# The head of the load queues: a first quarter of x in two token halves, and weight rows ahead of the DMA transposes

## Chip, cores, metric

One NeuronCore of one Trainium2 chip. The metric is the device time of one execution in microseconds (us). Kernels were timed in rounds beside the kernel before on the same chip.

## The reference

```python
# x (1, 2048, 1024), w_gate and w_up (1024, 3584), w_down (3584, 1024), all bf16
def reference(x, w_gate, w_up, w_down):
    return (_gelu(x @ w_gate) * (x @ w_up)) @ w_down   # gelu: the tanh form
```

## The kernel before

It computes the three products with a seven-product block scheme and is bound by TensorE for nearly the whole time. The change touches only the first 10 us: how the first 512 tokens of x and the first weight columns come in. The contraction has eight rows of 128 (`kd` 0 to 7). Rows 0 to 3 of x are loaded as they are, in two quarters of 256 columns, and transposed on TensorE; rows 4 to 7 come through DMA transposes. Weight columns 0 to 255 of a chunk come first (rows 0-1, 2-4, 5-7), columns 256 to 511 (here "the second column halves") after them.

```python
    FA = 2 * P
    first = (0, 0)
    load_x0(0, sp)                       # first quarter of x, 256 KB
    load_w(first, 0, 0, 2, act, 0, FA)   # gate rows 0-1 (j = 0 is gate, 1 is up)
    load_w(first, 1, 0, 2, sp, 0, FA)
    load_x0(1, act)                      # second quarter
    load_w(first, 0, 2, 5, act, 0, FA)
    load_w(first, 1, 2, 5, sp, 0, FA)
    act(nc.scalar.preload_act_table(ACT.Gelu_apprx_tanh))
    # ... (cut: identity)
    for i in range(NWARM):               # NWARM = 8 warm-up matmuls
        pe(nc.tensor.matmul(banks[i][:], lhsT=warm_l, rhs=warm_r, start=True, stop=True))

    for kd in range(KH, KD):             # x rows 4 to 7, one DMA transpose each
        load_xT(xT, 0, 0, kd, kd + 1)
        if kd == KH + 1:
            for j in range(2):
                load_w(first, j, 5, KD, act, 0, FA)
    for j in range(2):
        load_w(first, j, 0, KD, sp, FA, FG)   # the second column halves
    # ... (cut: second token block, next chunk)

    def first_units(hT):                 # columns 0-255, units 0 and 1
        wg, wu = chunks[first]
        held = (VB, RB)
        transpose_x0(0)                  # TensorE, rows 0 and 1; copies to SBUF on VectorE
        for kd, j in [(kd, j) for kd in range(KD) for j in range(2)]:
            for u in range(2):
                mm_gu(banks[held[u][j]], (wg, wu)[j], u, 0, kd)
            if (j, kd) == (1, 0):
                transpose_x0(1)          # rows 2 and 3; copies on VectorE and ACT
        for u in range(2):
            unit_out(hT, held[u], u, 0)
    # ... then unit 2 and 3: the second column halves
```

## Time and profile before

| | before |
|---|---|
| time, median of 3 runs (range) | 542.07 us (541.71 to 542.49) |
| span of the profiled execution | 539.7 us |
| first transposes on TensorE | 4.38 us |
| second transposes | 6.10 us |
| unit 2 begins | 13.07 us |

Times within a profile count from the start of its span. Where I give the start of one matmul or the landing of one load, it is from the records of the trace; a load has landed when the last of its engines has reported, and these reports come over up to 2.5 us. A line of a timeline gives start and length in us, the engine (PE TensorE's matmuls, PEld its weight loads, DVE VectorE, ACT ScalarE, SPq and ACTq the issuing of those two queues), the source line, the operation, what it writes <- reads, the shapes, how many, and in brackets the idle time before it and what ended that. One line that the readings below need is not in the prediction, the second transposes:

```profile
6.10 0.61 PE L302 MATMUL bank<-ident,w_mem 128*128 128x128 bf16 x8
```

### The profile page before, as it was taken

Reading aid. Unit: us, or ns where it says so; the run is one execution under the profiler, and the core shown is the slowest. Engines: PE = TensorE matmul, PEld = TensorE weight load, DVE = VectorE, ACT = ScalarE, POOL = GpSimd, SP = SyncE. Lnnn points to the kernel's source line nnn. Section 1 sums busy time; section 2 is a strip of 40 time slices with the busy share of each in tenths; the row PEclk is TensorE's granted clock in tenths of the full one; section 3 lists DMA queues with packets and bytes.
Section 4 is the critical chain, followed back from the end, with each engine's and each line's share of the span. In section 5 each row is a group of like instructions: output and inputs, shape, how many; then the busy total and the mean of one; then the engine's idle time right before and its main releaser. Section 6 shows DMA issues by size and latency. Waiting matters only on the chain.

```text
span 539.7 us, 7102 instructions
## 1 busy us (share of the span) xinstructions
PE 535.1 (99%) x2392; PEld 374.5 (69%) x2392; DVE 354.9 (66%) x466; ACT 258.9 (48%) x438; POOL 235.0 (44%) x206
## 2 busy tenths in 40 slices
PE   9999999999999999999999999999999999999997
PEld 3457777666776676767776677777777766866865
DVE  1767777787775997889574434444444469969951
ACT  2435555555555319216465555555555551452270
POOL 0197777777776000000056776666777730000000
PEclk9999999999999999999999999999999999999999
DMA  9928577696827876779950405041331466677946
GB/s 233 310 82 230 185 242 237 184 286 195 277 76 252 299 244 227 249 265 313 327 182 1 155 2 156 7 149 57 99 106 51 157 204 213 226 241 246 291 145 207
DMA packets 84771, 102.70 MB, mean 190 GB/s; under 512 B 18688, under 2 KB 66304, under 8 KB 84736
## 3 DMA queue, kind: packets, MB, share of 16 engines
q1 hardware_dynamic: 61936, 80.30, 46.2%
q10 hardware_dynamic: 22800, 21.96, 13.2%
q8 instruction: 19, 0.31, 0.2%
q14 instruction: 16, 0.13, 0.1%
HBM read 85.98 MB, written 12.58 MB: 183 GB/s over the span
## 4 chain that ended last, share of the span: by engine, by line
PE 98%; DMA 1%; ACTq 0%; ACT 0%; issue 0%
PE bank L386 61%; PE bank L656 33%; PE bank L252 5%; DMA w_mem<-in_w_gate_dram 1%; ACTq L161 0%; ACT xT L312 0%; ACT o_sb L709 0%; ACTq L167 0%; ACTq L709 0%
## 5 line engine op out<-in xcount | busy, mean ns | idle before, releaser
L386 PE MATMUL bank<-t_mem,s_mem 128*128 128x512 f32 x1016 | 239.8, 394 | 0.0
L386 PEld LDWEIGHTS bank<-t_mem,s_mem 128*128 128x128 f32 x1016 | 190.8, 188 | 41.9
L358 POOL TENSOR_TENSOR s_mem<-w_mem 128x512 fp32r<-128x512 bf16 x100 | 115.8, 1178 | 201.3 <-DMA w_mem<-in_w_up_dram 104.6
L276 DVE TENSOR_TENSOR hT<-w_mem,bank 128x512 bf16<-128x512 f32 x104 | 71.3, 686 | 92.4 <-PE bank L386 46.3
L656 PE MATMUL bank<-t_mem,s_mem 128*128 128x512 f32 x544 | 127.2, 392 | 0.0
L656 PEld LDWEIGHTS bank<-t_mem,s_mem 128*128 128x128 f32 x544 | 102.1, 188 | 22.2 <-issue 0.2
L409 DVE TENSOR_TENSOR bank<-bank,m 128x512 f32<-128x512 f32 x104 | 67.3, 694 | 46.9 <-ACT m L431 45.3
L386 PE MATMUL bank<-xT,w_mem 128*128 128x512 bf16 x416 | 94.3, 380 | 0.0
L271 ACT ACTIVATE w_mem<-bank 128x512 f32<-128x512 f32 x104 | 61.9, 596 | 57.7 <-DVE bank L409 32.7
L386 PEld LDWEIGHTS <-w_mem 128*128 128x128 bf16 x416 | 38.7, 98 | 49.7 <-issue 6.5
L566 DVE TENSOR_TENSOR t_mem<-w_mem 128x1024 fp32r<-128x1024 bf16 x56 | 65.5, 1216 | 0.0
L358 POOL TENSOR_TENSOR s_mem<-w_mem,s_mem 128x512 fp32r<-128x512 bf16 x50 | 62.1, 1267 | 0.0
L358 POOL TENSOR_TENSOR s_mem<-s_mem,w_mem 128x512 fp32r<-128x512 f32 x50 | 59.6, 1212 | 0.0
L371 ACT CAST s_mem<-w_mem 128x512 fp32r<-128x512 bf16 x52 | 32.0, 616 | 33.1 <-PE bank L386 29.1
L436 ACT COPY bank<-bank 128x512 f32<-128x512 f32 x52 | 29.6, 570 | 38.1 <-PE bank L386 38.1
L631 DVE TENSOR_TENSOR s_mem<-hT 128x512 fp32r<-128x512 bf16 x52 | 34.2, 685 | 10.2 <-PE bank L656 9.5
L656 PEld LDWEIGHTS <-hT 128*128 128x128 bf16 x224 | 21.3, 98 | 26.6 <-issue 2.1
L431 ACT COPY m<-bank 128x512 f32<-128x512 f32 x52 | 30.5, 587 | 17.1 <-PE bank L386 17.1
L440 ACT COPY bank<-bank 128x512 f32<-128x512 f32 x52 | 29.6, 570 | 13.5 <-PE bank L386 13.5
L709 ACT CAST o_sb<-bank 128x512 bf16<-128x512 f32 x28 | 15.4, 585 | 39.6 <-PE bank L656 39.6
L591 DVE TENSOR_TENSOR o_sb<-wd_sb,o_sb 128x512 fp32r<-128x512 bf16 x28 | 29.4, 1051 | 0.5
L252 PE MATMUL bank<-xT,w_mem 128*128 128x512 bf16 x128 | 28.4, 379 | 0.3 <-DVE xT L310 0.2
(42 smaller groups left out, 250.4 us busy)
## 6 DMA issues: line engine op xcount, KB each, us to landing
t_mem<-t_dram SPq DMA_DIRECT2D x56, 512.0 KB, 5.3
w_mem<-in_w_gate_dram ACTq DMA_DIRECT2D x10, 1024.0 KB, 5.6
w_mem<-in_w_up_dram ACTq DMA_DIRECT2D x10, 1024.0 KB, 9.1
wd_sb<-in_w_down_dram SPq DMA_DIRECT2D x28, 256.0 KB, 5.0
t_dram<-o_sb SPq DMA_DIRECT2D x28, 256.0 KB, 2.4
wd_sb<-in_w_down_dram SPq DMA_DIRECT2D x12, 512.0 KB, 8.8
w_mem<-in_w_down_dram SPq DMA_DIRECT2D x10, 512.0 KB, 6.1
w_mem<-in_w_down_dram SPq DMA_DIRECT2D x4, 1024.0 KB, 6.3
```

The source lines that it names most:

```text
L252: nc.tensor.matmul(ps[:], lhsT=w_sb[:, kd, fi * P : (fi + 1) * P], rhs=xT[tb][:, kd, :], start=(kd == 0), stop=(kd == KD - 1),)
L271: act(nc.scalar.activation(out=g_sb, in_=ps[:], func=ACT.Gelu_apprx_tanh))
L276: nc.vector.tensor_tensor(out=hT[:, fc, tb * TB : (tb + 1) * TB], in0=g_sb, in1=ps[:], op=ALU.mult,)
L358: pool(nc.gpsimd.tensor_tensor(out=t, in0=in0, in1=in1, op=op))
L371: act(nc.scalar.copy(out=t, in_=a(1, 1)))
L386: nc.tensor.matmul(banks[bank][:], lhsT=lhs[:, c, :], rhs=rhs[:, c, :], start=start and c == 0, stop=c == KH - 1, skip_group_check=True,)
L409: nc.vector.tensor_tensor(out=banks[dst][:], in0=banks[src][:], in1=m5[j][:], op=ALU.add)
L431: act(nc.scalar.copy(out=m5[j][:], in_=banks[V_[j]][:]))
L436: act(nc.scalar.copy(out=banks[RB[j]][:], in_=banks[QB[j]][:]))
L566: dve(nc.vector.tensor_tensor(out=t, in0=in0, in1=in1, op=ALU.subtract))
L631: dve(nc.vector.tensor_tensor(out=t, in0=in0, in1=in1, op=op))
L656: nc.tensor.matmul(banks[bset[u]][:], lhsT=lhs(i, u), rhs=rhs(i), start=start and i == 0, stop=stop and i == NS - 1, skip_group_check=True,)
```

## The change

The intent: start TensorE earlier, by giving each queue only half of the first quarter of x at its head, and keep ACT from stopping, by issuing weight rows 5 to 7 before the DMA transposes. One warm-up matmul is dropped, as real work should come sooner. To make room, the second quarter of x goes from second place on ACT to third on SP.

```diff
-    NWARM = 8
+    NWARM = 7
# ...
-    def load_x0(q, queue):
+    def load_x0(q, queue, ts0=0, ts1=TSB):
         eng = nc.scalar if queue is act else nc.sync
         cols = slice(q * XQ, (q + 1) * XQ)
-        src = x2[0:TB, cols].rearrange("(ts p) d -> p ts d", p=P)
-        queue(eng.dma_start(out=xs0[:, :, cols], in_=src))
+        src = x2[ts0 * P : ts1 * P, cols].rearrange("(ts p) d -> p ts d", p=P)
+        queue(eng.dma_start(out=xs0[:, ts0:ts1, cols], in_=src))
# ...
-    load_x0(0, sp)
+    load_x0(0, sp, 0, 2)
+    load_x0(0, act, 2, 4)
+    load_w(first, 1, 0, 2, sp, 0, FA)
     load_w(first, 0, 0, 2, act, 0, FA)
-    load_w(first, 1, 0, 2, sp, 0, FA)
-    load_x0(1, act)
+    load_x0(1, sp)
     load_w(first, 0, 2, 5, act, 0, FA)
     load_w(first, 1, 2, 5, sp, 0, FA)
+    for j in range(2):
+        load_w(first, j, 5, KD, act, 0, FA)
     act(nc.scalar.preload_act_table(ACT.Gelu_apprx_tanh))
 # ...
     for kd in range(KH, KD):
         load_xT(xT, 0, 0, kd, kd + 1)
-        if kd == KH + 1:
-            for j in range(2):
-                load_w(first, j, 5, KD, act, 0, FA)
```

## The prediction

> **What bounds the kernel now.** I read the page first: the busy shares and the chain that ended last, for how much of the time the change can touch at all. TensorE is busy for 535.1 of 539.7 us and is 98% of the chain; loads of the gate weights are 1%.
>
> ```profile
> span 539.7 us, 7102 instructions
> PE 535.1 (99%) x2392; PEld 374.5 (69%) x2392; DVE 354.9 (66%) x466; ACT 258.9 (48%) x438; POOL 235.0 (44%) x206
> PE 98%; DMA 1%; ACTq 0%; ACT 0%; issue 0%
> ```
>
> The change touches only loads issued before the loop and one warm-up matmul. So the second view is the timeline of the first 30 us. What the reader is to see: the warm-up matmuls, whose weight loads come every 0.43 us; the first real work at 4.38, when the first quarter of x has landed; the first weight matmul at 5.24; and, from 6.55 on, 107 matmuls in 23.74 us, or about 0.22 us each, which is nearly the gap of 0.216 us between two such matmuls that nothing holds up. From 10.9 us on no gap is left in the raw starts.
>
> ```profile
> 0.77 3.43 PE L202 MATMUL bank<-const-bfloat16-1.0 128*128 128x512 bf16 x8 [0.77 <-PEq L961]
> 2.29 5.12 SPq L172 DMA_TRANSPOSE xT<-in_x_dram  x4
> 4.38 0.62 PE L302 MATMUL bank<-ident,w_mem 128*128 128x128 bf16 x8 [0.18 <-DMA w_mem<-in_x_dram]
> 5.24 1.02 PE L252 MATMUL bank<-xT,w_mem 128*128 128x512 bf16 x4 [0.24 <-DVE xT L310]
> 6.55 23.74 PE L252 MATMUL bank<-xT,w_mem 128*128 128x512 bf16 x107
> 7.46 0.58 SPq L161 DMA_DIRECT2D w_mem<-in_w_gate_dram  x1
> 8.71 7.33 SPq L172 DMA_TRANSPOSE xT<-in_x_dram  x2
> ```
>
> Third, the chain in order of time for 0 to 15 us. What the reader is to see: the ACT queue stops. It issues gate rows 2 to 4 at 1.82, these land 5.65 us later at 7.47, only then does ACT issue the up rows 5 to 7 (7.50), and only behind that issue does ACT make the PSUM copy (7.98) that feeds the matmuls of row 3.
>
> ```profile
> 1.82 5.65 DMA w_mem<-in_w_gate_dram
> 7.50 0.44 ACTq L161
> 7.98 0.59 ACT xT L312
> 8.61 6.57 PE bank L252 x29
> ```
>
> Fourth, the waits from 4 to 14 us, to size what TensorE itself loses.
>
> ```profile
> PEld L252 <- DMA w_mem<-in_w_up_dram: 0.5, 1, 0.5
> PEld L252 <- DMA w_mem<-in_w_gate_dram: 0.4, 1, 0.4
> ```
>
> A weight load runs ahead of its matmul, so these waits are larger than what TensorE loses. From the single matmul starts against the 0.216 us step I get three holes: 0.12 before 7.53 (gate row 2), 0.21 before 8.61 (the ACT copy), 0.14 before 10.90 (up row 5). In sum **0.47 us**. That, and the start at 4.38, is all that this change can win: the later 510 us are TensorE back to back.
>
> **What the skill says, and whether the trace agrees.** "DMA: Bandwidth & Descriptors", Anatomy of one DMA: a transfer has a fixed part of about 2.0 us beside bytes over bandwidth. The trace agrees in kind: in the DMA view of the first microsecond 256 KB of x land after 3.6 us and 128 KB of gate after 3.4 us, so halving the bytes hardly shortens one. The same page, Issuing engines are not separate DMA queues: loads from SP and ACT run on the same 16 engines, and issuing on both saves only issue time. Issues here cost 0.45 to 0.58 us each, so that is what two halves at the heads of two queues may save. "TensorE: Matmul & The Clock Gate", Part 1: the array runs at half rate until a window of about 3.4 us has been busy, and the window is free-running. The trace agrees: warm-up steps are 0.43 us, twice 0.216, and the clock record goes to full at 3.92. The first page's Rules for kernel authors say that a transpose beside ordinary DMAs needs nothing; so the waits below are of the program's semaphores, not of the crossbar.
>
> **The change, part by part.**
> (a) The first quarter of x. Before, 256 KB led SP and 128 KB of gate led ACT; 384 KB had landed by 4.34. Now the two heads are 128 KB each and nothing else is ahead. The DMA view shows about 0.2 MB moved by 3.0 us and some 340 GB/s after that, so 256 KB have moved by about 3.2; the lag from bytes to landing is about 0.7. Estimate: 3.9 to 4.0, transposes at 3.95, **0.4 us earlier**. The first weights move to second place: issued at 1.24, landing after 3.5 as the second SP load does today, at 4.75. They are needed 0.86 us after the transposes (4.38 to 5.24 today), at 4.8, so they don't cost.
> (b) One warm-up matmul less: seven end at 0.77 + 7 x 0.43 = 3.8. Without this the eighth would hold TensorE until 4.2 and eat half of (a). Worth nothing by itself.
> (c) The second quarter goes from second on ACT to third on SP (issue 1.74 instead of 1.24). Needed after the first four matmuls, at 4.8 + 0.86 = 5.7; it landed at 5.5 with as many bytes ahead. No cost.
> (d) The last weight rows (5 to 7) on ACT before its table load. Gate rows go out at about 2.4 without a wait. All DMA landings of the trace come on eight semaphores, and an issue from the ninth on waits for the transfer eight before it: ACT's issue at 4.36 sits on the landing of x at 4.34, the one at 7.50 on that of gate rows 2 to 4 at 7.47. The up rows are now the ninth or tenth issue and wait for one of the two halves, until 4.0, not 7.5. So ACT is free by 5.8 (table load 1.28) for the copy needed near 7, and all **0.47 us** of holes go. First units alone could then end 0.4 + 0.47 = 0.9 us earlier: unit 2 at 12.2 instead of 13.07.
> (e) What it takes away. The four transposes of x rows 4 to 7 begin at 2.29 today. They now stand behind nine weight and x loads in the count of eight semaphores, so the first waits for a landing, until about 4.0, and four issues at 1.26 us (2.29 to 7.41 today) end at 9.1. Everything behind them on SP is 1.6 us later: the second column halves of gate and up, issued at 7.46 and 8.09 today, go at 9.1 and 9.7. They land 5.1 and 6.3 us after issue today, at 12.54 and 14.35, against use at 13.07 and 14.80: **0.53 and 0.45 us of slack**. They share the engines then with 192 KB of up rows that now go before, so they will be quicker: data start about 1.5 us after issue, 10.7, 512 KB at about 310 GB/s are 1.7 us, and 0.75 of lag, so gate at about 13.1 and up at about 14.85. These are estimates from the trace's packets.
>
> The sum: TensorE reaches unit 2 at 12.2 but its weights at 13.1, and the up half at 14.85 instead of 14.80. The 0.9 us won in (a) and (d) become a wait for the second column halves. **Net about 0, by my central estimate a gain of 0.1 to 0.2 us**, as the 1.6 us delay may be partly hidden in the queue. Later parts have room: the second x block, some 1.6 us later, lands near 18 and 20, for use at 19.98 and 20.84; GpSimd's first sums, started by weights that come at 22.8 and 25.8, end their second step at 31.85 for use at about 36.
>
> **The rivals.**
> 1. The gain is kept. The transposes don't wait, or the second halves are limited by bandwidth and not by issue, so that bytes moved earlier bring them earlier. For it: 16 engines show 250 to 310 GB/s almost without a hole from 2 to 14 us. Against it: their data start right behind the last transposes (9.5), which are held by 1.26 us each of issue. It would give up to 0.9 us: 541.2.
> 2. The wait moves and grows. The last transposes come late (issue at 7.8 plus the 3.7 us of today is 11.5, needed at 11.3) and the second halves come with the whole 1.6 us: 14.1 and 15.9, against 13.07 and 14.80. That costs 1.1 us: 543.2.
> 3. The clock. Seven warm-ups and a pause of 0.15 us may miss the window, and TensorE runs at half rate for up to another 3.4 us: at most 1.7 us lost, 543.8. For it: the flip at 3.92 is only 0.16 after the seventh ends. Against it: nine tenths of the window are busy. I give it one in ten.
> 4. Nothing of it, in that 3.8 us of warm-up and the DMA's fixed part hold the start: transposes at 4.2 or later. Then the start gives 0.2.
>
> **The range and the chances.** The centre is 542.07 - 0.15 = 541.9. Three runs before lie 0.8 us apart, and rivals 1 and 2 stand 0.9 below and 1.1 above; with weights of a quarter and a sixth the range of 8 in 10 is 541.1 to 542.9. Two per cent are 10.8 us, more than the whole 8.6 us up to row 3's matmuls, and all holes I found are 0.9; only a mistake such as a lost overlap in the later 500 us could do that. So same 0.99, faster 0.005, slower 0.005.
>
> **What would show it.** In the changed profile: transposes near 3.95 and first weight matmul near 4.8 (a); the ACT copy near 7 and no hole before rows 2, 3 and 5 (d); the first DMA transpose at about 4.0 and the second column halves issued about 9.1 (e); and a wait of weight loads for gate or up just before units 2, of 0.5 us or more. It is wrong if that wait is missing and TensorE reaches unit 2 near 12.2 (rival 1), if it stands at rows 6 and 7 (rival 2), or if matmul steps after 4 us are 0.43 us (rival 3).

## The result, and the profile after

| | before | after |
|---|---|---|
| time, median of 4 runs (range) | 542.28 us (541.71 to 542.76) | 542.90 us (542.53 to 543.79) |
| ratio after/before, 95% interval | | 1.0013 (0.9993 to 1.0033) |
| span of the profiled execution | 539.7 us | 540.7 us |

A ratio is the mean time of one kernel's runs over that of the other's of the same rounds, so it is not quite the ratio of the medians. The interval holds 1: by time alone the change is "same". The median stands at the very top of my range, 1.0 above its centre, and where I forecast a gain of 0.15 us there is a loss of about 0.6. The traces say more than the times.

The timeline of the changed kernel, lines that answer to those of before:

```profile
0.77 3.14 PE L205 MATMUL bank<-const-bfloat16-1.0 128*128 128x512 bf16 x7 [0.77 <-PEq L961]
...
3.72 5.11 SPq L172 DMA_TRANSPOSE xT<-in_x_dram  x4
...
3.75 1.07 PE L302 MATMUL bank<-ident,w_mem 128*128 128x128 bf16 x8
...
4.87 1.48 PE L252 MATMUL bank<-xT,w_mem 128*128 128x512 bf16 x4
...
6.47 0.62 PE L302 MATMUL bank<-ident,w_mem 128*128 128x128 bf16 x8
...
7.13 0.58 ACT L312 COPY xT<-bank 128x512 bf16<-128x512 bf16 x1 [1.45 <-PE bank L302]
8.88 0.58 SPq L161 DMA_DIRECT2D w_mem<-in_w_gate_dram  x1
...
13.54 10.75 PE L252 MATMUL bank<-xT,w_mem 128*128 128x512 bf16 x49 [0.21 <-DMA w_mem<-in_w_gate_dram]
```

The first transposes come 0.63 us earlier (3.75 against 4.38) and ACT's copy comes at 7.13, not 7.98. But the second transposes come 0.37 us later (6.47 against 6.10), and unit 2 begins at 13.54 against 13.07, after a wait for the gate half. The start gained 0.63 us, yet by unit 2 the kernel is 0.47 us behind.

The chain in order of time (of the whole run; its first part) shows what released unit 2. In the kernel before it ran through ACT's stopped queue; here it runs through SP's transposes, and ACT is gone from it:

```profile
0.74 2.96 DMA w_mem<-in_x_dram
3.70 0.02 issue
3.72 1.22 SPq L172
...
7.57 1.26 SPq L172
8.83 0.04 issue
8.88 4.62 DMA w_mem<-in_w_gate_dram
13.50 0.05 issue
13.54 20.90 PE bank L252 x96
```

The first DMA transpose waits for the first half of x (landed at 3.70), four issues follow, then the gate half of the second columns, 4.62 us in flight.

The table by stretches tells the same from the DMA side (the last two columns are the busy share of the DMA engines, which can pass 1, and GB/s). First the kernel before, then the changed one:

```profile
10.00:11.00 1.00, 1.00 (x6) 0.30 (x5) 0.00 (x0) 0.00 (x0) 0.00 (x0) 1.00 1.14 324
```

```profile
10.00:11.00 1.00, 1.00 (x6) 0.42 (x5) 0.00 (x0) 0.00 (x0) 0.00 (x0) 1.00 0.63 80
```

Between 10 and 11 us the engines move 80 GB/s, not 324. So bandwidth did not hold the gate half back there: it had been issued late, at 8.88, and by the packets of the trace its data came in bulk only from about 10.6.

Behind unit 2 the two traces run in step until 129 us, where the changed kernel loses another 0.41 us (0.47 becomes 0.88 at the last matmul). The waits from 125 to 131 us have one line there that the kernel before lacks, VectorE waiting for the store of a staged transpose:

```profile
DVE o_sb L591 <- DMA x_dram<-o_sb: 1.9, 1, 1.9
```

### The profile page after: what moved, and what is told of

Same layout as the page of the kernel before. It is cut to its first block, busy times and chain, and to the rows that moved or that the text cites. A ratio compares the mean times of both kernels' runs of the same rounds, so it can differ in the third digit from the quotient of the medians.

```text
span 540.7 us, 7104 instructions
## 1 busy us (share of the span) xinstructions
PE 535.9 (99%) x2391; PEld 374.7 (69%) x2391; DVE 356.5 (66%) x466; ACT 258.7 (48%) x438; POOL 235.1 (43%) x206
## 4 chain that ended last, share of the span: by engine, by line
PE 93%; DMA 4%; DVE 1%; SPq 1%; issue 0%; ACT 0%; DVEq 0%; ACTq 0%
PE bank L386 56%; PE bank L656 33%; PE bank L252 4%; DMA o_sb<-in_x_dram 2%; SPq L172 1%; DMA w_mem<-in_w_gate_dram 1%; DVE o_sb L591 1%; DMA w_mem<-in_x_dram 1%; DMA t_dram<-o_sb 0%; DMA x_dram<-o_sb 0%; DVE s_mem L631 0%; DVE bank L409 0%; ACT o_sb L709 0%; SPq L593 0%; ACT w_mem L271 0%
```

## The experiments

Theories at the start: **A**, the second column halves come late since the transposes ahead of them on SP wait for one of eight semaphores; **B**, the missing warm-up matmul delays the full clock; **C**, the loss at 129 us belongs to the change. After the first four runs came **D**: the second quarter of x comes late because of its new place. Twelve kernels were run; all gave correct results.

### after_again: the changed kernel unchanged

> The changed kernel once more, unchanged, for what repeats. Theory A (the second column halves of gate and up come late, because the DMA transposes ahead of them on SP wait for one of eight semaphores): first transpose issued near 3.7 us, halves at 8.9 and 9.5, gate half landing near 13.5, a hole of 0.3 to 0.5 us before unit 2, in this profile too. Rival B (the clock goes full at 5.8 instead of 3.9 because a warm-up matmul is missing): the flip is near 5.8 again; if it was only the phase of the window, it will stand elsewhere between 3.8 and 7.2. Rival C (a wait near 129 us costs 0.4 us more because staging is late): the same step of +0.4 there again. Time 1.000 to 1.003 of the kernel before.

Ratio 1.0016 (0.9989 to 1.0042). Issue of transposes and halves repeats: 3.62, 8.98. But unit 2 has no hole in front of it and begins at 14.37, 1.3 us later than before. The loss sits in another place, in front of the second transposes. Timeline:

```profile
4.71 1.04 PE L252 MATMUL bank<-xT,w_mem 128*128 128x512 bf16 x4 [0.30 <-DMA w_mem<-in_w_gate_dram]
7.63 0.45 PEld L302 LDWEIGHTS <-w_mem 128*128 128x128 bf16 x8 [2.38 <-DMA w_mem<-in_x_dram]
7.63 0.62 PE L302 MATMUL bank<-ident,w_mem 128*128 128x128 bf16 x8 [1.89 <-DMA w_mem<-in_x_dram]
```

TensorE is done with its first four matmuls by 5.75 and stands 1.89 us until the second quarter has landed (7.59). In the first profile the same load landed at 6.42, but the half-rate clock stretched the first matmuls to 6.35 (1.48 us instead of 1.04), so most of the wait was hidden: the fourth matmul began at 5.97, one step of 0.216 later TensorE could have gone on, and it went on at 6.47, so about 0.28 us were seen. That is the term I had put at zero. The gate half then lands at 13.95, before TensorE needs it: the two losses don't add, the longer one counts. The clock went full at 3.79 here, so the 5.80 of the first profile was not fixed by the seven matmuls.

### after_w8: eight warm-up matmuls

```diff
-    NWARM = 7
+    NWARM = 8
```

> The change with eight warm-up matmuls as before. Theory A: no difference at unit 2: its first matmul stays near 13.5, since it waits for a landing; TensorE just waits a little longer or shorter there. Rival B: if the missing matmul delays the clock, the flip is back at 3.9, the first units end 0.4 to 0.9 us earlier, but unit 2 starts at 13.5 all the same if A holds; only if A is false does the time fall by 0.5 us or more.

Ratio 1.0007 (0.9983 to 1.0030). Clock full at 4.26. Second quarter landed at 6.95, a wait of 0.92 us at the second transposes (7.00); gate half at 13.75, unit 2 at 13.80 with a hole of 0.30. As A says, an early clock doesn't help: unit 2 begins when the gate half lands.

### after_fa_act: the second column halves on ACT

```diff
         load_w(first, j, 5, KD, act, 0, FA)
+    for j in range(2):
+        load_w(first, j, 0, KD, act, FA, FG)
     act(nc.scalar.preload_act_table(ACT.Gelu_apprx_tanh))
 # ...
-    for j in range(2):
-        load_w(first, j, 0, KD, sp, FA, FG)
```

> The change with the second column halves of gate and up moved from SP (behind the DMA transposes) to ACT (behind rows 5 to 7, ahead of the table load). Theory A (issue-bound): they are issued near 4.4 to 5.5, land before 12, the hole before unit 2 is gone and unit 2 starts at 12.3 to 12.9, so 0.6 to 1.2 us earlier than in the changed kernel; or the hole moves to rows 4 to 7, if the transposes now come late. Bandwidth rival: the sum of bytes is the same, the halves still land at 12.5 to 13.5 and rows 4 to 7 come later than now, so nothing is won or some is lost.

A miss, and the largest loss: ratio 1.0063 (1.0040 to 1.0086). The timeline:

```profile
5.02 0.37 ACTq L161 DMA_DIRECT2D w_mem<-in_w_gate_dram  x1
...
8.96 0.43 ACTq L161 DMA_DIRECT2D w_mem<-in_w_up_dram  x1
...
10.72 0.58 ACT L312 COPY xT<-bank 128x512 bf16<-128x512 bf16 x1
...
11.36 3.61 PE L252 MATMUL bank<-xT,w_mem 128*128 128x512 bf16 x16 [1.56 <-ACT xT L312]
15.42 1.89 PE L252 MATMUL bank<-xT,w_mem 128*128 128x512 bf16 x8 [0.45 <-DMA xT<-in_x_dram]
```

ACT's second issue waits for a semaphore until 8.96, the table load and the copy behind it come late (the copy at 10.72) and hold TensorE by 1.56 us. The last transpose, issued at 8.39 instead of 7.57 and now in flight beside the halves, lands only at 15.38, too late for row 7. The gate half, issued at 5.02, needed 7.7 us and landed at 12.72. So an early issue alone did not bring it before 12 here. Why it needed 7.7 us stays open: bandwidth alone doesn't explain it, as the DMA view shows mostly 35 to 185 GB/s from 7.2 to 9 us, against 280 to 360 from 5.2 to 7.1.

### after_rows_back: rows 5 to 7 back behind the second transpose

```diff
-    for j in range(2):
-        load_w(first, j, 5, KD, act, 0, FA)
     act(nc.scalar.preload_act_table(ACT.Gelu_apprx_tanh))
 # ...
         load_xT(xT, 0, 0, kd, kd + 1)
+        if kd == KH + 1:
+            for j in range(2):
+                load_w(first, j, 5, KD, act, 0, FA)
```

> The change with rows 5 to 7 put back behind the second DMA transpose, the halves of x kept at the heads of the queues. Theory A: only seven loads stand before the first transpose, so it is issued near 2.8 without a wait and the second near 4.0; the second column halves go near 7.9, land near 12.6, and unit 2 starts at 12.6 to 13.1, some 0.5 to 0.9 us before the changed kernel. If what costs is the split of x itself (second quarter late, landing at 6.4), then unit 2 stays at 13.3 or later.

Ratio 1.0004 (0.9978 to 1.0029). SP's timeline:

```profile
2.80 5.11 SPq L172 DMA_TRANSPOSE xT<-in_x_dram  x4
...
7.96 0.58 SPq L161 DMA_DIRECT2D w_mem<-in_w_gate_dram  x1
```

With seven loads ahead the first transpose needs no semaphore back and goes at 2.80, the halves at 7.96; the gate half lands at 12.87 and unit 2 begins at 13.03 without a hole. That is A's forecast, but for a gate half 0.3 us later than its 12.6. The start is as early as in the changed kernel (3.71), yet unit 2 is only 0.04 us before that of the kernel before: at half rate until 6.42, the first four matmuls took 1.79 us and the second transposes began at 6.49. The second quarter, landed at 6.05, held nothing here.

### before_again: the kernel before unchanged

> The kernel before once more, for what repeats. If the second quarter of x lands late in the changed kernels because of its place in the queues (theory D), it lands here by 5.8 on its last engine again (5.52 in the first profile; 6.05 to 7.59 in five profiles with the new order). If it is just how the engines straggle on a given execution, it lands here anywhere from 5.5 to 7.5. Second column half of gate issued near 7.5, landing near 12.5, no hole before unit 2; unit 2 at 12.9 to 13.6. Clock flip anywhere from 3.8 to 7.2.

Ratio 0.9986 (0.9961 to 1.0011). Second quarter at 5.65, second transposes at 6.25, halves issued at 7.45, gate half at 12.36, no hole, unit 2 at 12.77. D's number; and the spread of the kernel before at unit 2 is at least 0.3 us, as gate rows 2 to 4 happened to land early and ACT held nothing.

### before_rows: only rows 5 to 7 ahead of the transposes

```diff
     load_w(first, 1, 2, 5, sp, 0, FA)
+    for j in range(2):
+        load_w(first, j, 5, KD, act, 0, FA)
     act(nc.scalar.preload_act_table(ACT.Gelu_apprx_tanh))
 # ... and taken out behind the second transpose
```

> The kernel before with only one part of the change: weight rows 5 to 7 issued ahead of the DMA transposes; x whole, eight warm-ups. Theory A: the first transpose waits for a landing until about 4.1 to 4.4, the second column halves go at 9.3 to 9.6 and the gate half lands near 13.8; no hole at rows 3 and 5, but one of 0.5 us or more before unit 2, which starts near 13.8, so this part alone costs 0.5 to 0.8 us. Second quarter of x lands by 5.8 (theory D: its place is the old one). If the loss were of the split of x only, unit 2 would start at 12.6 here.

Ratio 0.9985 (0.9964 to 1.0006). Partly a miss: here the first transpose still got a free semaphore (it was the seventh or eighth issue) and went at 2.30, only the second waited, until 4.24. The halves went at 8.12, 0.67 later than before, the gate half landed at 12.97, unit 2 began at 13.28 and waited for nothing. The second quarter, in its old place, landed at 5.63, as D wants. What held TensorE back was the clock, at half rate until 6.38. So this part alone costs nothing that shows, but its delay uses up most of the slack of the halves (gate landed at 12.97; the kernel before used it at 13.07).

### x1_act: the second quarter third on ACT

```diff
-    load_x0(1, sp)
+    load_x0(1, act)
```

> The change with the second quarter of x moved back to the ACT queue (third there), nothing else. Theory D by place: it has 256 KB ahead in its ring still, so it lands at 5.8 to 6.5, hardly better; by straggling beside the deeper ACT queue: it lands at 5.4 to 5.7. Theory A: second halves issued near 8.4 to 8.9, hole before unit 2 stays; unit 2 near 13.0 to 13.6.

A miss: ratio 1.0003 (0.9978 to 1.0028). It lands at 7.14, later than either forecast, its first engine as late as 6.26; TensorE waits 1.28 us at the second transposes (7.19) and unit 2 begins at 13.83, though the gate half, issued at 7.75, had landed at 12.77. Third place is late on ACT too, though not alike: here all engines are late, on SP mainly the last ones (below).

### x1_split: the second quarter in halves, third on both queues; rows 5 to 7 back

```diff
-    load_x0(1, sp)
+    load_x0(1, sp, 0, 2)
+    load_x0(1, act, 2, 4)
 # rows 5 to 7 as in after_rows_back
```

> The second quarter of x split in two token halves as well, third on each queue, and rows 5 to 7 back behind the second transpose. Theory D: each ring has only 256 KB ahead and 128 KB of it, so the quarter lands by 5.6, and with a warm clock the second transposes of TensorE run right after the first four matmuls, near 5.6 to 5.8. Eight loads are then ahead of the first DMA transpose, which waits until 3.7 (theory A), so the second halves go at 8.9 and unit 2 starts at 13.2 to 13.6 all the same. If A is wrong, unit 2 starts at 12.2 to 12.6.

Ratio 1.0009 (0.9985 to 1.0034). The halves land at 5.89 and 6.26, the earliest but one of the third places, though later than I expected; TensorE's second transposes run from 5.93, the last six from 6.31. Eight loads are ahead, the first transpose waits until 3.97, the halves go at 9.13, and the timeline has the hole before unit 2 again:

```profile
13.70 1.41 PEld L254 LDWEIGHTS <-w_mem 128*128 128x128 bf16 x8 [0.74 <-DMA w_mem<-in_w_gate_dram]
13.70 2.55 PE L254 MATMUL bank<-xT,w_mem 128*128 128x512 bf16 x11 [0.25 <-DMA w_mem<-in_w_gate_dram]
```

With D nearly mended, unit 2 still waits for the gate half: A alone is enough to hold it until 13.70.

### after_xt2: two DMA transposes of two rows instead of four of one

```diff
-    for kd in range(KH, KD):
-        load_xT(xT, 0, 0, kd, kd + 1)
+    for kd in range(KH, KD, 2):
+        load_xT(xT, 0, 0, kd, kd + 2)
```

> The changed kernel with its four DMA transposes of one x row each joined into two of two rows. The later transposes of four rows take 1.6 to 2.3 us to issue where nothing blocks them, so two of two rows should take some 3 us or less instead of 5.1. Theory A (the second column halves are late by their issue, landing 4.5 to 5.1 us after it, in nine profiles): first transpose still waits until near 3.7, the halves go by about 6.5 instead of 8.9, the gate half lands before 12.0, and no hole is left before unit 2. Theory D: the second quarter of x still lands at 6.0 to 7.6, so unit 2 starts at 12.6 to 13.9. If landing is bound by bandwidth instead, the gate half still lands at 12.8 or later.

A miss in size. Ratio 1.0009 (0.9993 to 1.0024). The second transpose took 3.30 us to issue, so the halves went at 7.98, not 6.5, and the gate half landed at 13.37; rows 4 and 5 came as one transfer at 10.74, a wait of 0.76 us for TensorE; unit 2 began at 14.2 (worked out from ACT's third gelu less 1.93 us, as this trace lacks some matmul records). The second quarter landed at 6.77, so D holds; A is not tested by it, since little of the issue time went away.

### x1_second: the second quarter second on SP

```diff
+    load_x0(1, sp)
     load_w(first, 1, 0, 2, sp, 0, FA)
     load_w(first, 0, 0, 2, act, 0, FA)
-    load_x0(1, sp)
```

> The changed kernel with the second quarter of x put second on SP, ahead of the first up rows; nothing else. Theory D (place in the ring: 128 KB ahead as in the kernel before, not 256 KB): it lands at 5.2 to 5.8 on its last engine; the first up rows, third now, land at 5.6 to 6.5 and TensorE waits up to 1 us for them instead. If it straggles for another reason, it lands at 6.0 to 7.6 as in the other new orders. Second halves issued near 8.9, landing near 13.5, unit 2 near 13.5.

Ratio 1.0016 (1.0003 to 1.0029). It lands at 5.25, the earliest of all, with everything else of the change in place. So one place further up mends it, as D says. The price stands in the timeline:

```profile
5.52 1.89 PE L252 MATMUL bank<-xT,w_mem 128*128 128x512 bf16 x4 [0.73 <-DMA w_mem<-in_w_gate_dram]
...
7.20 1.06 PE L302 MATMUL bank<-ident,w_mem 128*128 128x128 bf16 x8
```

The first gate rows now land at 5.47 instead of 4.8, TensorE stands 0.73 us, and its clock stays at half rate until 9.93 (the four matmuls take 1.89 us, the transposes 1.06). Unit 2 begins near 15.0, not near 13.5 as expected. Whether the pause caused the late clock, one profile can't say.

### before_x1_late: only the place of the second quarter

```diff
-    load_x0(1, act)
     load_w(first, 0, 2, 5, act, 0, FA)
+    load_x0(1, act)
```

> The kernel before with one thing of the change alone: the second quarter of x goes from second to third place in its queue (ACT), behind gate rows 2 to 4; x whole, eight warm-ups, rows 5 to 7 where they were. Theory D (place): it lands at 6.2 to 7.3 on its last engine instead of 5.5 to 5.7, TensorE waits 0.4 to 1.3 us before its second transposes (they begin at 6.3 to 7.4 instead of 6.10), and unit 2 starts at 13.2 to 14.0 instead of 12.8 to 13.1. If place doesn't matter and the head halves make the engines straggle, it lands by 5.8 and unit 2 starts at 12.7 to 13.1.

Its interval lies just above 1, as that of x1_second does: ratio 1.0027 (1.0004 to 1.0049); with a bound of 2% both count as the same. From the timeline:

```profile
5.39 1.29 PE L252 MATMUL bank<-xT,w_mem 128*128 128x512 bf16 x4
...
6.99 0.62 PE L302 MATMUL bank<-ident,w_mem 128*128 128x128 bf16 x8 [0.32 <-DMA w_mem<-in_x_dram]
```

It lands at 6.95, the second transposes wait for it until 6.99 (6.10 before), and unit 2 begins at 13.50. With nothing else of the change, the new place makes the load late by 1.4 us. Two things keep this from being the lateness of the changed kernel: the clock, at half rate until 5.96, would have put the second transposes at about 6.5 by itself, and here the load has 192 KB more ahead of it in all, not only in its queue, so that already its first engine is 1.6 us late (6.77 against 5.17).

### before_xt2_dve: a version meant to beat both

The kernel before with two-row transposes, rows 5 to 7 issued behind both of them, and row 3's copy on VectorE.

```diff
-    for kd in range(KH, KD):
-        load_xT(xT, 0, 0, kd, kd + 1)
-        if kd == KH + 1:
-            for j in range(2):
-                load_w(first, j, 5, KD, act, 0, FA)
+    for kd in range(KH, KD, 2):
+        load_xT(xT, 0, 0, kd, kd + 2)
+    for j in range(2):
+        load_w(first, j, 5, KD, act, 0, FA)
 # ...
-            if q == 0 or n == 0:
+            if True:
```

> A version meant to beat both: the kernel before, with its queue heads and second quarter as they are, the four DMA transposes joined into two, and the PSUM copy for row 3 on VectorE instead of ACT, so that a blocked ACT queue holds no matmul. Theory: second quarter of x lands by 5.7; no hole before row 3; second halves issued by about 6.0, gate half landing by 11.5; rows 4 and 5 of x may come later as one transfer, needed at 9.4. Unit 2 starts at 12.4 to 12.8, 0.3 to 0.6 us before the kernel before; time 0.998 to 1.000 of it, which the timing alone can't resolve here.

Not resolved. Median 541.81 beside 542.42 of the kernel before, five of six runs between 541.1 and 544.7, one at 547.59; ratio 1.0016 (0.9981 to 1.0052). Halves issued at 6.70, gate half landed at 12.45 (5.8 us in flight, so no earlier than before), unit 2 at 12.8. It is not shown to beat the kernel before.

### All looks side by side

One profile each; us from the start of the span. "Place" is that of the second quarter of x in its queue. Unit 2 of x1_second, after_xt2 and before_xt2_dve is worked out from ACT's third gelu.

| kernel | place | it lands | second transposes | gate half issued | lands | unit 2 | clock full |
|---|---|---|---|---|---|---|---|
| before | 2, ACT | 5.52 | 6.10 | 7.46 | 12.54 | 13.07 | 3.92 |
| before_again | 2, ACT | 5.65 | 6.25 | 7.45 | 12.36 | 12.77 | 4.22 |
| before_rows | 2, ACT | 5.63 | 6.79 | 8.12 | 12.97 | 13.28 | 6.38 |
| before_xt2_dve | 2, ACT | 5.54 | 6.24 | 6.70 | 12.45 | 12.8 | 4.79 |
| x1_second | 2, SP | 5.25 | 7.20 | 9.26 | 14.16 | 15.0 | 9.93 |
| before_x1_late | 3, ACT | 6.95 | 6.99 | 7.45 | 12.54 | 13.50 | 5.96 |
| after_rows_back | 3, SP | 6.05 | 6.49 | 7.96 | 12.87 | 13.03 | 6.42 |
| x1_act | 3, ACT | 7.14 | 7.19 | 7.75 | 12.77 | 13.83 | 3.97 |
| after | 3, SP | 6.42 | 6.47 | 8.88 | 13.49 | 13.54 | 5.80 |
| after_w8 | 3, SP | 6.95 | 7.00 | 8.89 | 13.75 | 13.80 | 4.26 |
| after_again | 3, SP | 7.59 | 7.63 | 8.98 | 13.95 | 14.37 | 3.79 |
| x1_split | 3, both | 5.89, 6.26 | 5.93, 6.31 | 9.13 | 13.66 | 13.70 | 5.27 |
| after_xt2 | 3, SP | 6.77 | 6.82 | 7.98 | 13.37 | 14.2 | 5.47 |
| after_fa_act | 3, SP | 7.40 | 7.45 | 5.02 (ACT) | 12.72 | 16.28 | 5.21 |

Five looks at second place: 5.25 to 5.65. Eight looks at an unsplit third place: 6.05 to 7.59. The ranges don't touch.

## Why the prediction was wrong

Two steps failed. Each alone is enough to undo the gain, and which of them ends last differs from look to look.

**The last term of (e), the flight of the second column halves.** In the profile beside the result, unit 2 began 0.05 us after the gate half had landed, so this term set it. The mechanism was right: the first transpose waited for a landing, the halves were issued late, and unit 2 got a hole. The size was not. I let the flight shrink from 5.1 us to 4.0, as the halves would have less company. It took 4.62 us (4.86 and 4.97 in after_w8 and after_again). So the gate half, though issued at 8.88 and not 9.1, landed at 13.49 and not 13.1, and a loss of 0.47 us stood at unit 2 where I had none.

**(c)**, "It landed at 5.5 with as many bytes ahead. No cost." It landed at 6.42 to 7.59 in three looks (after, after_again, and after_w8 with eight warm-ups). The cost at the second transposes was about 0.28 us in the first profile, 0.92 in after_w8 and 1.89 in after_again, and in the last of these it, and not the gate half, set unit 2. I counted the bytes issued ahead over both queues, 512 KB in both kernels. This fits its first engine: it reported at 5.27, against 5.17 before. It fails for the last one, at 6.42 against 5.52. In the six looks at third place on SP, unsplit (after, after_again, after_w8, after_fa_act, after_rows_back, after_xt2), the first engine reported at 4.90 to 5.42, and the last one 0.6 to 2.5 us after it, against 0.35 in the kernel before.

That the new place makes the load late is shown: one place further up mends it (x1_second), and the ranges of the table don't touch. By what it does so is in part argued. In the kernel before, 128 KB stood ahead of it in ACT's queue, now 256 KB in SP's. The Trainium skill's "DMA: Bandwidth & Descriptors", Queues, rings and completion order, fits: each engine takes turns between the queues' rings, packet by packet, and consumes one ring in order; I quoted the same page for the shared engines and left this out. The packets of the traces, counted without regard to the engine (they don't name it), agree: when as many bytes of its queue had gone out as end with this load, both queues together had moved 806 to 828 KB in the four looks at second place on ACT, 868 to 931 KB at third on SP, 1005 in x1_act, 1200 in before_x1_late and 628 in x1_second. So before_x1_late and x1_second move more than the place in one queue: in both, the bytes in its own queue, those in all and the moment of issue (1.75 instead of 1.24 in the change) move together. By the same count these bytes were out 0.3 to 0.8 us later than before; the rest of the loss on SP is the tail of late engines. Why some engines lag so is not settled.

**Right: (a)**, in kind and nearly in size. Transposes at 3.75 instead of 3.95 as forecast; gain 0.63 instead of 0.4. First gate rows at 4.82 (forecast 4.75), first weight matmul at 4.87 (4.8). One reading was wrong: 3.6 us for 256 KB and 3.4 us for 128 KB were of two loads in flight together, and don't say that halving the bytes hardly shortens one. The two halves landed 2.96 and 3.22 us after their issue.

**(b)**, worth nothing: after_w8 shows no gain from the eighth. Rival 3, the clock, is real: the record goes to full between 3.79 and 9.93 in fourteen profiles. It does so before 4.3 in three of six with eight warm-ups and in two of eight with seven; that it has to do with the change is not shown, and so few looks don't rule it out. In the first profile after, it stretched the first matmuls, but that cost nothing more, as what came next wasn't there sooner: the second quarter landed at 6.42 and the second transposes began at 6.47.

**Right: (d)**, in kind. ACT copies at 7.13, off the chain, no hole before rows 2, 3 and 5; a new one of 0.20 before row 4, for the first DMA transpose (9.67), which I had not listed. "The transfer eight before it" is not exact: in the kernel before, the up rows' issue at 7.50 sat on gate rows 2 to 4, five issues earlier.

**The rest of (e)**. First transpose 3.72 (about 4.0), halves 8.88 and 9.50 (9.1 and 9.7), gate half 13.49 (13.1), hole 0.37, up half 15.22 against its use at 15.27 (14.85). after_rows_back took the semaphore wait away and the hole went; x1_split brought it back. Over the looks where SP issues the gate half from 7.4 to 9.3, it lands 4.5 to 5.4 us later; issued at 6.70 or 5.02 it takes 5.8 or 7.7 and lands no earlier than 12.4. So a later issue means a later landing above 7.4; below, something else holds it, and what is open.

**The sum.** I had: 0.9 us gained, 0.9 lost to the halves, net a gain of 0.15. But my own terms came to a loss of 0.03 to 0.05 (gate half at 13.1 against 13.07, up half at 14.85 against 14.80); the gain was an allowance for a delay "partly hidden in the queue", with nothing measured behind it. Measured at unit 2: a loss of 0.47, 0.7 and 1.3 us in three looks (after, after_w8, after_again) against the first profile of before. The losses of (c) and (e) don't add, since a TensorE that is late for its second transposes is no longer early for the halves. So mending one alone gives nothing: x1_split still waits for the gate half until 13.70, and x1_act, whose gate half is there at 12.77, still begins unit 2 at 13.83.

**Rival 2** put the growing wait at rows 6 and 7 and at unit 2, 1.1 us in all; nearest in size, but its place at rows 6 and 7 is wrong (0.20 at row 4 is all). **Open:** the 0.41 us at 129 us. A hole there shows in after, after_again (1.8), after_w8 (0.3), after_xt2 (0.4), and in before_rows (0.6), which has only (d); not in before, before_again, nor in the other seven kernels. VectorE waits there for a store of staged x that comes behind the next chunk's weights (two loads of 1 MB), and the second one's landing differs by 1.6 us between two looks (121.08 in before, 122.66 in after). Whether the change brings it on or the executions do, these runs don't tell; holes of 0.4 to 0.7 us stand later, between 226 and 495 us, in six of the profiles, of kernels with and without the change (before_again at 227, after_rows_back at 466). Nor do the times alone establish that the change is slower: both its intervals hold 1. Each look is one profile, so what is said of 0.1 or 0.2 us between two kernels is no more than that.

## What to carry to other kernels

When loads at the head of a kernel are reordered, note for each its place in its own queue besides the bytes ahead in total, and ask of the last engine, not of the first. Count the issues too: with the eight completion semaphores of this program the ninth load waits for an earlier one, and a queue whose issues are slow (DMA transposes, 1.26 us each) passes that wait on to everything behind it. A gain at the start is worth only what the next transfer in line leaves of it. And where a forecast lets a transfer become quicker, as I did for the halves, take the measured flight instead until a trace shows otherwise.

## What the Trainium skill lacked or had wrong

- "DMA: Bandwidth & Descriptors" gives the order within a ring but no size for what one place costs between two busy queues: here 256 KB at second place landed by 5.25 to 5.65 us, at third by 6.05 to 7.59.
- The same page has the issue of a DMA transpose only in sequencer cycles, for small tiles, and no time for these shapes: here 1.1 to 1.3 us for 128 x 512 elements on SP, mostly 0.4 to 0.6 us for a plain load; the two-row transpose took 1.34 us when first and 2.97 to 3.30 us when second.
- No page says by how much the 16 engines of one load drift apart: the reports of one 256 KB load came over 0.35 us in the kernel before and 2.5 us in after_again.
- "TensorE: Matmul & The Clock Gate", Part 1, puts the change to full rate around 4 us of activity, give or take 0.5, and explains that the window runs free. First matmuls stood at 0.77 to 0.78 us in all fourteen profiles; full rate came 3.0 to 5.7 us after that in thirteen and 9.2 in one, a wider spread. TensorE was not busy throughout in these first microseconds (it paused for loads), so this is no contradiction; the page's figure just doesn't carry over to such a start.
